# A spectral filter and two MLPs on one core: the bias written into PSUM by ScalarE, the second mixing unit in three passes, four weight conversions in the forward transform

## The chip, the core and the metric

One core of a Trainium2 chip runs the whole program in one launch. The metric is the device time of one execution in microseconds (us). The kernel before takes 1150.15 us, the median of 3 runs (1149.65 to 1151.89). TensorE (PE) multiplies, with its weight loads shown apart as PEld; VectorE (DVE), ScalarE (ACT) and GpSimd (POOL) do the elementwise work; SyncE (SP) and POOL issue DMAs.

## The reference

The input is x of shape (2, 3008, 256). Its real Fourier transform along the sequence is mixed by a complex 256x256 weight with a complex bias, soft-thresholded and transformed back; two MLPs follow (256 to 2048 to 256), one after the other.

```python
X = np.fft.rfft(x, axis=1)
Yr = Xr @ w_r - Xi @ w_i + b_r
Yi = Xr @ w_i + Xi @ w_r + b_i
Y = sign(Y) * maximum(abs(Y) - 0.01, 0)      # real and imaginary part apart
y = np.fft.irfft(Y, n=3008, axis=1)
h = x @ w_in;  x = (h * sigmoid(1.702 * h)) @ w_out       # first MLP
h = x @ w_in2; x = (h * sigmoid(h)) @ w_out2              # second MLP
```

## The kernel before

**Order.** The instructions of each engine run in the order in which the program issues them: every region opened by `region(...)` has an order written out by hand. So an instruction that waits on ACT, DVE or POOL holds back whatever stands behind it on that engine.

**Stages.** The forward transform (to some 59 us) is a product of the folded input with cosine and sine matrices, in 16 groups `(q, b, t)`: `q` is the parity of the folded rows, `b` the batch, and `t` tells even or odd frequencies (`p = t // 2`) and cosine or sine (`cs = t % 2`). The first four groups run in two pairs (`fwd_pair`), and then the loop of line 524 runs groups 4 to 15: `fwd_mm(g)` on PE, `fold(g + 3)` on DVE, the evacuation of the group before (`fwd_evac`, ACT and DVE), and, for the `g` of the list `tf`, a `tick`. `fold` and `halves` add and subtract pieces of the input; with `t == 0` both halves, sum and difference, are made (lines 323 to 337), although the difference is first read by `t == 1`. Groups 12 to 15 are evacuated through a copy `eo` on ACT (line 450) and four additions on DVE (L461, L462, L436). Every group takes two PSUM banks of a pool of four, one pool for even and one for odd groups (`bank`).

**Mixing** (59 to 131 us). Twelve units `(b, p, j)` of 128 frequencies, in `mid_mm(i)`, each with two sums of 512 columns, in the same PSUM pools. The first two units (`n32 = 2`) multiply fp32 by fp32, 16 matmul records each. The others run in three passes of fp32r with the operands split in a high and a low part: `xh` and `xl` (`xsplit`, ACT, and for `xl` a POOL DMA that adds), `wh` (L556, ACT) and `wl` (L557, DVE); 24 matmuls each. A 25th matmul, `ones` by `bias_hl` (L578), adds the bias to the first sum. `xsplit(i + 3, 1)` and `xsplit(i + 2, 0)` run two to three units ahead. `wh`, `wl` and the first splits stand after the last forward evacuation (lines 555 to 557).

**Conversion of the first MLP's weights.** They come as 64-bit numbers. One conversion is: load of 256 KB into the single buffer `raw64` (`cv_load`); absolute value on ACT (L180) into the single buffer `cv_c`; five DVE instructions (L185 to L189); a POOL DMA that adds `cv_c` to `cv_a` (L190); and, once that landed, the placing: four DVE additions (L218 to L221), four ACT instructions (L105, L107, twice) and two POOL DMAs (L106). A `tick` issues L180 of the next conversion first, then the placing of the one before, then L185 to L190, then the next load. Conversions run at `g` 6, 10 and 13 of the forward loop (`tf`), at the units of `tm` (0, 2, 4, 6, 8, 10) and at step 3 of the inverse transform (`ti`). What is converted in the later ones is kept (`hold`) and placed at the steps `pl` of the inverse.

**Inverse and MLPs.** The inverse (131 to 175 us) has 16 steps. Then 2 layers x 6 blocks of 1024 tokens x 8 weight groups run in `group`. Each group computes seven products in three passes (a Strassen-like scheme), with sums `xb[l, i, k]` of the block's quarters that are made in the last group of the block before (`xprep`). Inside `group`, `y1` is copied out of bank X by ACT (L895), and the product `prod(X, 4, 3, False)` may only be added to X once that is done; `y2` is finished by L926 and `y3` by L930. L796, `xtmp = b21 - src`, is the last step of `xprep(3)`; it reads the quarter `b11` that L895 of the next block overwrites.

Of the kernel before, what the change touches and what calls it, by code (L numbers as in the profile page):

```python
# [56 lines left out]
def spectral_mlp_kernel(ctx, tc, xin, mfwd, minv, wc, bias, w_in1, w_out1, w_in2, w_out2, outT):  # L57
# [61 lines left out]
    m_order = [("f", q, t) for q, t in ((0, 0), (0, 1), (1, 0), (1, 1), (1, 2), (1, 3), (0, 2), (0, 3))] + [("i", q, t) for q in range(2) for t in (0, 2)]  # L119
# [49 lines left out]
    def cv_bits(raw, n):  # L169
# [110 lines left out]
    raw_p = opened("raw", "left", 3)  # L280
    lv_p = opened('lv', 'left', N('lvb'))
# [20 lines left out]
    def halves(q, b, j, cs):  # L302
# [6 lines left out]
        else:  # L309
            lv = lv_p.tile([P, 2, D], F32, tag="lv", name="lv")  # L310
# [4 lines left out]
    def fold(g):  # L315
# [33 lines left out]
    def fold_pair(g):  # L349
        q, b, _ = groups[g]  # L350
        for j in range(NJ):
# [7 lines left out]
            if b == 0:  # L359
                load_raw()  # L360

    def load_wc():
        raws["wc"] = raw_p.tile([P, 4, D], F32, tag="raw", name="wc_f")
        nc.sync.dma_start(out=raws["wc"], in_=wc.rearrange("p k (h d) -> p (k h) d", h=2))
        nc.sync.dma_start(out=bias_f[0:1], in_=bias)

    def prep_wc():
# [5 lines left out]
        nc.vector.tensor_sub(bias_lo, bias_f[0:1], r32(bias_hl[0:1]))  # L373
        nc.gpsimd.dma_start(out=bias_hl[1:2], in_=bias_lo)
# [102 lines left out]
    bias_lo = wc_p.tile([1, 2 * D], F32R, name="bias_lo")  # L477
# [37 lines left out]
    load_raw(3)  # L515
# [8 lines left out]
    for g, (q, b, t) in enumerate(groups):  # L524
# [33 lines left out]

    def mid_mm(i):
# [4 lines left out]
        for grp in range(2):  # L564
            t = bank(i, "psm")
            n = 0

            for xi, off in ((0, 0), (3, D)) if grp == 0 else ((1, 0), (2, D)):
                for mm in range(2):
                    w = slice(off, off + 2 * D)  # L570
                    if hl is None:
                        nc.tensor.matmul(t, x[xi][:, mm], wc_s[:, mm, w], start=(n == 0), stop=(n == 3 and grp == 1))  # L572
                    else:
                        for k, (st, mv) in enumerate(passes(hl[xi][0][:, mm], hl[xi][1][:, mm], wh[:, mm, w], wl[:, mm, w])):
                            nc.tensor.matmul(t, st, mv, start=n == 0 and k == 0, stop=n == 3 and grp == 1 and k == 2)  # L575
                    n += 1
            if grp == 0:
# [43 lines left out]

    post = thr = None
# [27 lines left out]
    hold.insert(2, hold.pop())  # L650
# [123 lines left out]

    def xprep(l, i, k, part=3):
# [398 lines left out]
```

## Time and profile before

| | |
|---|---|
| median of 3 runs | 1150.15 us |
| the profiled execution, its own time | 1149.84 us |
| its span, first to last instruction | 1148.0 us |
| PE, PEld busy | 1138.8 us (99%), 946.3 us (82%) |
| ACT, DVE, POOL busy | 774.1, 615.5, 475.9 us (67%, 54%, 41%) |
| chain that ended last: PE | 93% |
| granted TensorE clock, mean | 1.000 |

The span is the time between the first and the last instruction, and 1.84 us of the execution lie around it. Times in the rows are microseconds from the span's start, durations of single instructions on a page are in ns. PE's ends are modelled, since matmuls overlap: the pace of matmuls is read from how far pieces of the chain lie apart and not from the length of one. A bracket after an instruction gives the idle time of its engine before it and what ended that. Short gaps on PE only show in the timeline; an engine that idles elsewhere costs nothing by itself.

### The profile page before, as it was taken

How to read it: one execution, taken by the hardware profiler on the slowest of the kernel's cores; microseconds unless marked ns; L12 is line 12 of the kernel's file. 1: busy time of each engine (PE TensorE's matmuls, PEld its weight loads, DVE VectorE, ACT ScalarE, POOL GpSimd, SP SyncE). 2: the span in 40 equal slices, each digit the busy share in tenths (PEclk: the TensorE clock that was granted, in tenths of full speed). 3: DMA queues.
4: the chain of work that ended last, by engine and by line, in shares of the span. 5: the costliest groups of instructions: out<-in, count | busy, mean ns of one | idle time of the engine just before them, and what ended most of it. 6: DMA issues, size and time to landing. Idle time of an engine off the chain costs nothing.

```text
span 1148.0 us, 14644 instructions
## 1 busy us (share of the span) xinstructions
PE 1138.8 (99%) x5094; PEld 946.3 (82%) x5094; DVE 615.5 (54%) x1015; ACT 774.1 (67%) x1445; POOL 475.9 (41%) x410
## 2 busy tenths in 40 slices
PE   8999999999999999999999999999999999999998
PEld 6768987878888888888889878888888888888897
DVE  8889997764565465564554633533523523523422
ACT  2587357877677676686677776765765866757655
POOL 0253164443444444444447646433334433344333
PEclk9999999999999999999999999999999999999999
DMA  8699494431121212112211000010000100100100
GB/s 306 176 185 238 114 161 86 105 72 37 49 62 37 74 37 59 52 38 74 52 41 37 28 28 19 1 38 1 20 18 1 37 1 1 38 1 1 37 1 33
DMA packets 39852, 68.69 MB, mean 60 GB/s; under 512 B 3681, under 2 KB 16225, under 8 KB 39778
## 3 DMA queue, kind: packets, MB, share of 16 engines
q1 hardware_dynamic: 26306, 45.51, 12.2%
q0 software_dynamic: 13472, 22.24, 11.4%
q8 instruction: 40, 0.66, 0.2%
q14 instruction: 34, 0.28, 0.1%
HBM read 35.15 MB, written 10.35 MB: 40 GB/s over the span
## 4 chain that ended last, share of the span: by engine, by line
PE 93%; DVE 2%; ACT 2%; issue 1%; DMA 1%; SPq 0%; POOL 0%; DVEq 0%; ACTq 0%; POOLq 0%
PE o L848 43%; PE x L876 37%; PE psm L575 5%; PE psi L394 4%; PE psf L394 3%; PE psm L572 1%; ACT yt L879 1%; DMA xr<-in_x 1%; ACT g L881 0%; DVE keep L313 0%; DVE tmp L796 0%; ACT yt L895 0%; ACT x L783 0%; DVE x L790 0%; SPq L485 0%
## 5 line engine op out<-in xcount | busy, mean ns | idle before, releaser
L886 POOL TENSOR_TENSOR g<-yt,g 128x512 fp32r<-128x512 f32 (+1 forms) x282 | 363.6, 1301 | 498.2 <-PE x L876 306.3
L848 PE MATMUL o<-g,wo 128*128 128x512 f32 (+1 forms) x2304 | 559.7, 385 | 0.0
L876 PE MATMUL x<-x,wi 128*128 128x512 f32 (+1 forms) x2016 | 498.9, 386 | 2.0 <-ACT yt L895 1.1
L848 PEld LDWEIGHTS o<-g,wo 128*128 128x128 f32 x2304 | 432.5, 188 | 80.6
L876 PEld LDWEIGHTS x<-x,wi 128*128 128x128 f32 x2016 | 377.5, 188 | 77.1 <-ACT yt L895 3.2
L879 ACT ACTIVATE yt<-yt 128x512 f32<-128x512 f32 (+1 forms) x288 | 179.1, 622 | 264.2 <-DVE yt L926 217.3
L881 ACT CAST g<-yt 128x512 fp32r<-128x512 f32 (+1 forms) x384 | 235.0, 612 | 12.2
L926 DVE TENSOR_TENSOR yt<-yt,x 128x512 f32<-128x512 f32 (+1 forms) x96 | 64.8, 675 | 217.7 <-PE x L876 217.3
L898 DVE TENSOR_TENSOR yt<-yt,x 128x512 f32<-128x512 f32 (+1 forms) x96 | 65.0, 677 | 175.0 <-ACT yt L895 173.1
L886 DVE TENSOR_TENSOR g<-yt,g 128x512 fp32r<-128x512 f32 (+1 forms) x102 | 70.0, 686 | 71.9 <-ACT g L881 71.9
L190 POOL DMA_DIRECT2D cv_a<-cv_c x32 | 28.1, 878 | 112.4 <-DVE cv_c L189 106.0
L930 DVE TENSOR_TENSOR yt<-yt,x 128x512 f32<-128x512 f32 (+1 forms) x96 | 64.9, 676 | 0.0
L790 DVE TENSOR_TENSOR x<-yt,x 128x512 fp32r<-128x512 f32 (+1 forms) x55 | 47.6, 866 | 31.5 <-ACT x L783 31.5
L895 ACT COPY yt<-x 128x512 f32<-128x512 f32 (+1 forms) x96 | 54.9, 572 | 1.7 <-DVE tmp L796 0.9
L879 ACT ACTIVATE yt<-x 128x512 f32<-128x512 f32 (+1 forms) x96 | 56.0, 584 | 0.0
L916 ACT COPY yt<-x 128x512 f32<-128x512 f32 (+1 forms) x96 | 55.9, 582 | 0.1
L914 ACT COPY yt<-x 128x512 f32<-128x512 f32 (+1 forms) x96 | 54.9, 572 | 1.4 <-PE x L876 1.4
L394 PE MATMUL psi<-m,f 128*128 128x188 f32 (+3 forms) x224 | 45.2, 357 | 0.0
L394 PEld LDWEIGHTS psi<-m,f 128*128 128x128 f32 x224 | 37.6, 190 | 5.5
L394 PE MATMUL psf<-m,xf 128*128 128x190 f32 (+2 forms) x176 | 36.2, 367 | 1.4 <-ACT xt L446 0.8
L394 PEld LDWEIGHTS psf<-m,xf 128*128 128x128 f32 x176 | 29.6, 190 | 8.3 <-ACT xt L446 1.3
L783 ACT CAST x<-yt 128x512 fp32r<-128x512 f32 (+1 forms) x59 | 36.4, 617 | 0.0
(120 smaller groups left out, 804.8 us busy)
## 6 DMA issues: line engine op xcount, KB each, us to landing
raw<-in_wi SPq DMA_DIRECT2D x32, 256.0 KB, 3.6
cv_a<-cv_c POOLq DMA_DIRECT2D x32, 256.0 KB, 5.0
raw<-in_wo SPq DMA_DIRECT2D x16, 512.0 KB, 3.9
xl<-xt POOLq DMA_DIRECT2D x20, 256.0 KB, 8.0
out_t<-yt SPq DMA_DIRECT2D x20, 256.0 KB, 2.0
raw<-in_x SPq DMA_DIRECT2D x9, 512.0 KB, 5.6
wi<-tmp POOLq DMA_DIRECT2D x8, 256.0 KB, 4.7
w_in<-cv_a SPq DMA_DIRECT2D x8, 256.0 KB, 2.0
```

Source lines behind the costliest of these rows:

```text
L394: nc.tensor.matmul(ps, hi[:, c : c + P], m[:, k, :w], start=i == 0, stop=i == last)
L575: nc.tensor.matmul(t, st, mv, start=n == 0 and k == 0, stop=n == 3 and grp == 1 and k == 2)
L848: nc.tensor.matmul(acc[h, mm], st, mv, start=first and k == 0, stop=last and k == 2)
L876: nc.tensor.matmul(ps, st, mv, start=first and m == 0, stop=m == 2, skip_group_check=True)
L879: nc.scalar.activation(g, g if src is None else src, func)
L881: nc.scalar.copy(gh, g)
L886: eng.tensor_sub(gl, g, r32(gh))
L895: nc.scalar.copy(y1, X)
L898: nc.vector.tensor_add(y1, y1, Y)
L916: nc.scalar.copy(y3, X)
L926: nc.vector.tensor_add(y2, y2, X)
L930: nc.vector.tensor_add(y3, y3, Z)
```

## The change

- Mixing: `n32` goes from 2 to 1, so unit 1 runs in three passes too. `xsplit(1, 1)` stands at group 10, `xsplit(2, 1)` and `xsplit(1, 0)` right behind `wl`. For units 4 to 11 ACT copies the bias from `bias_f` into the bank of the first sum one unit ahead (`put_bias`), the first matmul adds onto it (`start=False`), and the bias matmul is left out. The bias array is now 128 rows; its load of 256 KB stands at group 9, the small buffer `bias_lo` is gone.
- Forward: groups run with `t` in the order 0, 2, 1, 3; the difference half is made only when `t == 1` comes, in place in the raw tile; raw tiles 5 instead of 3, `lv` 3 instead of 6; loads are issued in another order, the last raw tile after `fold(7)`.
- Conversions: `tf` is 6, 10, 12, 14 instead of 6, 10, 13, and `ti` is empty, so four fall in the forward transform, six in the mixing, none in the inverse; `pl`, the order of `hold` and the buffers of `cv_a` follow.
- MLPs: for every block but the first L796 moves from the end of `xprep(3)` to a new `hook(7)` behind L926; `preload_act_table(AF.Silu)` stands in the first group of layer 1, behind L895.

```diff
-'tf': [6, 10, 13], 'ti': [3], 'pl': [1, 4, 8, 10, 13], 'n32': 2
+'tf': [6, 10, 12, 14], 'ti': [], 'pl': [1, 4, 8, 9, 11, 13], 'n32': 1
-    groups += [(1, b, t) for b in range(B) for t in range(4)]
+    groups += [(1, b, t) for b in range(B) for t in (0, 2, 1, 3)]
-            lv = lv_p.tile([P, 2, D], F32, tag="lv", name="lv")
+            lv = raws[q, b, j][1] if cs else lv_p.tile([P, 2, D], F32, tag="lv", name="lv")
-            if t == 0:
-                halves(q, b, j, 0)
+            if q == 1 and t < 2:
+                halves(q, b, j, t)
...
-            if t == 0:
-                halves(q, b, j, 1)
...
-    load_raw(3)
+    load_raw(6)
+    load_m()
+    load_m()
+    load_raw(2)
...
+        if g == 4:
+            load_raw()
...
+        if g == 9:
+            nc.sync.dma_start(out=bias_f, in_=bias)
         if g == 10:
-            xsplit(N('n32'), 1)
+            xsplit(1, 1)
...
     nc.vector.tensor_sub(wl, wc_s, r32(wh))
+    xsplit(2, 1)
+    xsplit(1, 0)
...
-            t = bank(i, "psm")
+            ready = i in filled and grp == 0
+            t = filled.pop(i) if ready else bank(i, "psm")
...
-            if grp == 0:
+            if grp == 0 and not ready:
                 nc.tensor.matmul(t, ones, bias_hl, start=False, stop=True)
...
+    def put_bias(i):
+        if 4 <= i < len(mids):
+            filled[i] = bank(i, "psm")
+            nc.scalar.copy(filled[i], bias_f)
...
         sd = mid_sd(*post) if post is not None else None
+        put_bias(i + 1)
...
-            if k == 3:
-                nc.vector.tensor_sub(xtmp[0], b21, src)
+            if k == 3 and not begun:
+                xfifth(l, i, src)
...
         nc.vector.tensor_add(y2, y2, X)
+        hook(7)
...
+                if h == 7:
+                    xfifth(*nxt)
...
+            if (l, i, p, h) == (1, 0, 0, 1):
+                nc.scalar.preload_act_table(AF.Silu)
```

## Rows read from the trace of the kernel before

**Rows 1.** Part 1 of the page: busy time, share of the span, instructions.
```profile
PE 1138.8 (99%) x5094; PEld 946.3 (82%) x5094; DVE 615.5 (54%) x1015; ACT 774.1 (67%) x1445; POOL 475.9 (41%) x410
```

**Rows 2.** Chain in order of time, mixing: start us, us, what.
```profile
59.59 3.43 PE psm L572 x8
...
63.25 6.87 PE psm L572 x16
...
99.51 5.45 PE psm L575 x24
...
105.19 5.45 PE psm L575 x24
...
130.63 4.39 PE psi L394 x27
```

**Rows 3.** Timeline of DVE, 18 to 25 us: start us, us, instruction, [idle before].
```profile
18.78 0.69 DVE L313 TENSOR_TENSOR lv<-raw 128x512 f32<-128x512 f32 x1
...
23.50 0.42 DVE L332 TENSOR_TENSOR xf<-lv 128x256 f32<-128x256 f32 x1
```

**Rows 4.** Timeline of PE, the same stretch.
```profile
23.98 1.24 PE L394 MATMUL psf<-m,xf 128*128 128x190 f32 x6 [0.63 <-DVE xf L332]
```

**Rows 5.** Timeline of DVE, 30 to 64 us.
```profile
44.92 0.29 DVE L218 TENSOR_TENSOR tmp<-cv_a 128x128 f32<-128x128 f32 x1 [1.65 <-DMA cv_a<-cv_c]
...
45.86 0.42 DVE L185 TENSOR_SCALAR cv_c<-cv_c 128x512 f32<-128x512 f32 x1
...
55.71 0.43 DVE L185 TENSOR_SCALAR cv_c<-cv_c 128x512 f32<-128x512 f32 x1
...
58.43 0.42 DVE L461 TENSOR_TENSOR xt<-psf,eo 128x256 f32<-128x256 f32 x1
...
61.55 1.76 DVE L557 TENSOR_TENSOR wl<-wc_s,wh 128x1536 fp32r<-128x1536 f32 x1
```

**Rows 6.** Timeline of ACT, 30 to 68 us.
```profile
55.00 0.68 ACT L180 ACTIVATE cv_c<-raw 128x512 f32<-128x512 f32 x1 [2.54 <-DMA raw<-in_wi]
...
57.44 0.83 ACT L450 COPY eo<-psf 128x376 f32<-128x376 f32 x2
...
60.04 1.48 ACT L556 CAST wh<-wc_s 128x1536 fp32r<-128x1536 f32 x1
...
62.47 1.12 ACT L507 CAST xh<-xt 128x512 fp32r<-128x512 f32 x2
64.64 0.68 ACT L180 ACTIVATE cv_c<-raw 128x512 f32<-128x512 f32 x1 [1.05 <-DMA raw<-in_wi]
```

**Rows 7.** Instructions on the tile psm: ns min/median/max, first and last start us.
```profile
L584 ACT COPY us<-psm x12: 559/568/580, 67.1 to 128.0; 128x512 f32<-128x512 f32 x12
```

**Rows 8.** Instructions of line 796, the same columns.
```profile
L796 DVE TENSOR_TENSOR tmp<-yt x11: 621/686/1786, 255.1 to 1065.9; 128x512 f32<-128x512 f32 x9, 128x448 f32<-128x448 f32 x2
```

**Rows 9.** Timeline of DVE, 247 to 272 us.
```profile
252.34 0.68 DVE L930 TENSOR_TENSOR yt<-yt,x 128x512 f32<-128x512 f32 x1
...
255.05 1.79 DVE L796 TENSOR_TENSOR tmp<-yt 128x512 f32<-128x512 f32 x1
```

**Rows 10.** Timeline of POOL, 244 to 272 us.
```profile
255.00 2.97 POOL L886 TENSOR_TENSOR g<-yt,g 128x512 fp32r<-128x512 f32 x2 [5.32 <-ACT g L881]
```

**Rows 11.** Timeline of PE, 247 to 272 us.
```profile
252.48 2.35 PE L876 MATMUL x<-x,wi 128*128 128x512 f32 x9
...
257.57 0.96 PE L876 MATMUL x<-x,wi 128*128 128x512 f32 x3 [0.69 <-ACT yt L895]
```

**Rows 12.** Timeline of PE, 636 to 674 us.
```profile
658.95 0.96 PE L876 MATMUL x<-x,wi 128*128 128x512 f32 x3 [0.26 <-ACT yt L895]
...
663.04 1.97 PE L876 MATMUL x<-x,wi 128*128 128x512 f32 x6 [0.70 <-ACT yt L916]
```

**Rows 13.** Timeline of ACT, 636 to 674 us.
```profile
658.31 0.59 ACT L895 COPY yt<-x 128x512 f32<-128x512 f32 x1 [0.88 <-DVE tmp L796]
```

**Rows 14.** A stretch of the tail: us, PE, PEld, DVE, ACT, POOL busy, PEclk, DMA share, GB/s.
```profile
1147.00:1148.00 1.00, 0.00 (x0) 0.00 (x0) 0.00 (x0) 0.00 (x0) 0.00 (x0) 0.89 0.00 0
```

More of the change, by code (lines that the diff above doesn't have):

```diff
@@ L118, in spectral_mlp_kernel @@
     m_tiles = {}
-    m_order = [("f", q, t) for q, t in ((0, 0), (0, 1), (1, 0), (1, 1), (1, 2), (1, 3), (0, 2), (0, 3))] + [("i", q, t) for q in range(2) for t in (0, 2)]
+    m_order = [("f", q, t) for q, t in ((0, 0), (0, 1), (1, 0), (1, 2), (1, 1), (1, 3), (0, 2), (0, 3))] + [("i", q, t) for q in range(2) for t in (0, 2)]
     def load_m():
@@ L172, in cv_bits @@
         c = cv_p.tile([P, 2 * CU], F32, tag="c", name="cv_c", bufs=1)
-        if n < 4:
+        if n < 3:
             a = cv_p.tile([P, 2 * CU], F32, tag="a", name="cv_a", bufs=3)
-        elif n == 4:
+        elif n == 3:
             a = cv_p.tile([P, 2 * CU], F32, tag="ld", name="cv_a", bufs=1)
@@ L279, in spectral_mlp_kernel @@
     m0_p = opened("m0", "left", 4)
-    raw_p = opened("raw", "left", 3)
-    lv_p = opened('lv', 'left', N('lvb'))
+    raw_p = opened("raw", "left", 5)
+    lv_p = opened('lv', 'left', 3)
     xs_p = opened("xs", "left", 18)
     groups = [(0, b, cs) for b in range(B) for cs in range(2)]
-    groups += [(1, b, t) for b in range(B) for t in range(4)]
+    groups += [(1, b, t) for b in range(B) for t in (0, 2, 1, 3)]
     groups += [(0, b, 2 + cs) for b in range(B) for cs in range(2)]
@@ L358, in fold_pair @@
             del raws[q, b, j]
-            if b == 0:
-                load_raw()
     def load_wc():
@@ L364, in load_wc @@
         nc.sync.dma_start(out=raws["wc"], in_=wc.rearrange("p k (h d) -> p (k h) d", h=2))
-        nc.sync.dma_start(out=bias_f[0:1], in_=bias)
+        nc.sync.dma_start(out=bias_f[0:1], in_=bias[0:1])
     def prep_wc():
@@ L372, in prep_wc @@
         nc.scalar.copy(bias_hl, bias_f)
-        nc.vector.tensor_sub(bias_lo, bias_f[0:1], r32(bias_hl[0:1]))
-        nc.gpsimd.dma_start(out=bias_hl[1:2], in_=bias_lo)
+        nc.vector.tensor_sub(bias_f[0:1].bitcast(F32R), bias_f[0:1], r32(bias_hl[0:1]))
+        nc.gpsimd.dma_start(out=bias_hl[1:2], in_=bias_f[0:1].bitcast(F32R))
     xt = {}
@@ L476, in spectral_mlp_kernel @@
     bias_hl = wc_p.tile([P, 2 * D], F32R, name="bias_hl")
-    bias_lo = wc_p.tile([1, 2 * D], F32R, name="bias_lo")
     bias_f = wc_p.tile([P, 2 * D], F32, name="bias_f")
@@ L514, in spectral_mlp_kernel @@
     fold(5)
-    load_raw(3)
     for x in prev:
@@ L571, in mid_mm @@
                     if hl is None:
-                        nc.tensor.matmul(t, x[xi][:, mm], wc_s[:, mm, w], start=(n == 0), stop=(n == 3 and grp == 1))
+                        nc.tensor.matmul(t, x[xi][:, mm], wc_s[:, mm, w], start=n == 0, stop=n == 3 and grp == 1)
                     else:
                         for k, (st, mv) in enumerate(passes(hl[xi][0][:, mm], hl[xi][1][:, mm], wh[:, mm, w], wl[:, mm, w])):
-                            nc.tensor.matmul(t, st, mv, start=n == 0 and k == 0, stop=n == 3 and grp == 1 and k == 2)
+                            nc.tensor.matmul(t, st, mv, start=n == 0 and k == 0 and not ready, stop=n == 3 and k == 2 and (ready or grp == 1), skip_group_check=ready)
                     n += 1
-            if grp == 0:
+            if grp == 0 and not ready:
                 nc.tensor.matmul(t, ones, bias_hl, start=False, stop=True)
@@ L620, in mid_fold @@
                 ft[q, b, p, -1] = ft.pop((q, b, p, 0))
+    filled = {}
+    def put_bias(i):
+        if 4 <= i < len(mids):
+            filled[i] = bank(i, "psm")
+            nc.scalar.copy(filled[i], bias_f)
     post = thr = None
@@ L649, in spectral_mlp_kernel @@
     hold.extend(settle(True))
-    hold.insert(2, hold.pop())
+    hold[2:] = hold[4:] + hold[2:4]
     cv_load(1 - len(loaded))
@@ L773, in xsums, with xfifth @@
         E('xse', 1).tensor_sub(b12, b22, b12)
+    def xfifth(l, i, src=None):
+        (b11, _), (b21, _) = xhalves(i)
+        nc.vector.tensor_sub(xtmp[0], b21, b11 if src is None else src)
     def xprep(l, i, k, part=3):
@@ L1157 @@
         "in_wc": wc,
-        "in_bias": np.concatenate([inputs["b_r"], inputs["b_i"]])[None],
+        "in_bias": np.ascontiguousarray(np.broadcast_to(np.concatenate([inputs["b_r"], inputs["b_i"]]), (P, 2 * D))),
         "in_wi1": np.ascontiguousarray(inputs["moe_w_in"]).view(np.int64),
```

7 lines of the change are left out of this document (1 added, 6 removed).

## The prediction

> **What bounds the kernel now.** I read the busy shares first, then the chain of waits in order of time, and then the timeline of each engine where the change acts. PE is busy for 1138.8 of 1148.0 us [rows 1], so an edit can only gain by taking matmuls away or by closing one of PE's few gaps, and costs whatever new gap it makes on PE. The chain through the mixing is PE alone [rows 2]: two fp32 units from 59.59, then ten units whose pieces lie 105.19 - 99.51 = 5.68 us apart, and the inverse at 130.63. A difference of 0.2% (2.3 us) is about what a measurement of this kernel can tell from no change. The sum is made against the profiled execution, 1149.84 us (span 1148.0 and 1.84 around it), which lies 0.31 below the median of the runs.
>
> **Matmuls taken away.** Of the 5.68 us of a unit the 24 matmuls take 5.45 and the bias matmul the other 0.23 [rows 2]. Eight units lose it: 8 x 0.23 = 1.84 us. Unit 1 goes from 16 fp32 records to 24 in fp32r: in the chain 16 records are 6.87 us, 24 are 5.45 [rows 2], a gain of 1.42. Together -3.26 us of PE work. The bias write costs ACT a copy of some 0.57 us [rows 7] per unit, issued right behind the copy `us` of the unit before the running one, so about a unit ahead of its reader. It writes a bank whose last reader is four units back, so it waits for nothing but ACT's own queue, and I take it at nothing. The trace has no such write into PSUM; between nothing and 8 x 0.57 = 4.6 us, were ACT late in every unit, I take nothing, as ACT has waits of its own in every unit. A gain from the write itself is excluded, since it only adds work. The larger bias load is one more DMA on SP at group 9, between loads; nobody waits for it before unit 4.
>
> **Forward transform.** At group 4 PE waits for the third folded tile, `xf` at 23.50 on DVE, and starts again at 23.98 [rows 3, 4]. Three differences of 0.69 us stand between 18.78 and that tile [rows 3]; they move to `fold(6)`. Without them its chain loses 2.0 us, of which I give 0.9 back, because the sums and their followers then depend on each other directly and can't overlap: 1.1 us earlier on PE. The last raw tile is loaded only once `fold(7)` has freed a buffer, some 5.4 us after `fold(4)` ends near 22.8 (1.0 for `fold(5)`, 4.0 for `fold(6)`, which is as long as `fold(4)` from 18.78, and 0.4), and is due four groups later on PE. I take that at nothing; if it lands late, PE loses that time ahead of unit 1, where by the next paragraph some 5 us are idle anyway. So PE would leave the forward transform at some 58.4 instead of 59.6 (unit 0 at 59.59 [rows 2]).
>
> **The fourth conversion, and what it blocks.** A tick in the loop holds ACT until the conversion before has let its buffers go. That shows at group 13: ACT stood idle for 2.54 us before L180 at 55.00, and the evacuation copies `eo` ran only after it, at 57.44 [rows 6]. The conversions come in a fixed rhythm, because each needs the landing of the DMAs of the one before: L185 stands at 45.86 and 55.71 [rows 5], and the fourth L180 at 64.64 [rows 6]. Periods are 9.85 us and, from L180 to L180, 9.64. In the kernel before this fourth one is unit 0's, behind `wh` and the first splits. In the changed one it stands at group 14, ahead of the last two evacuations, `wh`, `wl` and the splits of unit 1, and it can come hardly sooner: the first two ticks stay where they are, all of DVE's work before the second is the same, and there DVE had only 1.65 us of slack [rows 5], of which later folds and their dependences use up most. I take 0.4 us earlier, so L180 at about 64.25.
> Behind it on ACT, from the rows: L180 and the placing 2.44 (55.00 to 57.44), two `eo` 0.83, `wh` and a pair `xl` 2.43 (60.04 to 62.47), then the first `xh` 0.56 (half of 1.12) [rows 6]: 64.25 + 6.26 = 70.5. On DVE: L185 to L189 2.72 (55.71 to 58.43), from 64.97 to 67.69; two evacuations of 1.04 each (three from 58.43 to 61.55), to 69.77; `wl` 1.76, to 71.5 [rows 5]. Unit 1's first pass needs `xh` and `wh`, its second `wl`. So after one matmul it runs from 71.5, as if it had started at 71.3 without a wait.
> On PE unit 0 starts near 59.2 (its bank waits for the evacuation of group 12, behind the third conversion) and ends 7.1 us later (two halves of 3.43 and the bias 0.23), at 66.3. PE idles for some 5 us. From unit 1 on: three units of 5.68 and eight of 5.45, 60.64 us, so the inverse starts at 131.9 instead of 130.63: **+1.3 us**, where without this wait the two stages would bring 1.1 + 3.26 = 4.4. Bounds: DVE using all its 1.65 us of slack, L180 near 62.6 after somewhat quicker landings, gives -0.4; landings slower by 0.55 in each of two periods, L180 at 65.35, +2.4. I take the middle, because the DMAs are the same ones.
> Moving the later conversions and placings (none in the inverse, one placing more there) costs nothing: the inverse is PE alone in the chain, DVE loses 3.7 us of work there (44.92 to 45.86 and 55.71 to 58.43 [rows 5]), and nothing is to be gained where PE doesn't wait. At worst PE waits for the two ACT copies of the added placing, 1.2 us by a copy's 0.57 [rows 7].
>
> **Block changes of the MLPs.** L796 takes 0.69 us in most blocks but up to 1.79 [rows 8], at 255.05 [rows 9], where POOL starts two subtractions at 255.00 [rows 10]. L895 of the next block may not overwrite L796's input, so PE waits: 0.69 us at 257.57 [rows 11], and with what lies in matmul overhead 0.96 us from start to start. At the change of layers ACT idles 0.88 us for L796 [rows 13], and PE waits 0.26 and 0.70 [rows 12]. In its new place, behind L926, POOL is idle (its 5.32 us of idle time end at 255.00 [rows 10]), so L796 takes 0.69. L930, from 252.34 to 253.02 [rows 9], moves behind it, and would end near 253.65. It frees the bank of the second product of the next block, the last three of the nine matmuls from 252.48 [rows 11], due at 252.48 + 6 x 0.23 = 253.85: covered, with 0.2 us left. Without that cover each us of delay is a us of PE. Gain: 0.96 at the first, 0.88 at the change of layers (ACT's chain moves by just its idle time), together **-1.85 us**, between -1.2 and -2.3. The preload of the table takes nothing off ACT's queue, where the load stood behind L895 before too: nothing.
> The Trainium skill (SBUF — State Buffer, Who interferes with whom) says that a DVE instruction with two SBUF inputs and a GpSimd instruction that reads SBUF exclude each other for a whole instruction. The rows at 255 agree. By that rule a POOL instruction in the new place would make L796 1.79 again, L930 about 1.2 us later still, and give about 1 us of the 1.85 back; the trace has POOL idle there.
>
> **Sum.** +1.3 - 1.85 = -0.55: 1149.3 against the profile, 1149.6 against the median. Own range with the bounds above: 1147.4 to 1151.4, or 1147.7 to 1151.7 against the median.
>
> **Rivals.**
> 1. *No wait at unit 1*: the conversions come quicker, or ACT isn't held. Then 4.4 + 1.85 = 6.25 us are gained: 1143.9. For it speaks only that DVE has its folds behind it sooner; against it the L180 of rows 6, which stood 2.54 us for a landing. A partial case (L180 near 61, unit 1 some 3 us sooner than I say) gives about 1146.6.
> 2. *The clock falls in the idle piece*, and the kernel is slower. The only long idle time of PE before is the tail: no matmul runs in its last us, 1147 to 1148, and the granted clock of that us is 0.89 [rows 14], so in it TensorE went from 2.4 to 1.2 GHz. If that happens at 66 to 71 us, unit 1 starts at half pace; at the lower level each us costs 0.5 us, and for 3 us of it, which I take between nothing and the 5 us of the idle piece, as no row shows a stretch at the lower level behind one, 1.5 us are lost: 1151.1. The point from which this decides: with a fallen clock the change is slower by over 0.2% if the fourth L180 comes after 65.6, without it only after 67.1.
> The Trainium skill (TensorE: Matmul & The Clock Gate, Part 1) calls the lower level the default that activity lifts; the tail agrees, and the rule stands against every edit that opens a gap on PE.
> 3. *L796 only moves its wait*: L930 becomes late in its new order and PE waits at the second product. Then the MLP gain is under 0.9 us, 1150.6.
>
> **How the numbers follow.** Forecast with rival 3 0.40, clock fallen 0.22 (of that 0.08 over the bound), rival 1 whole 0.18, partial 0.13, something new elsewhere 0.07 (0.05 of it slower). Faster by over 0.2% (under 1147.85): 0.18 + 0.13 + 0.02 = 0.33; slower (over 1152.45): 0.08 + 0.05 = 0.13; within: 0.54. The range takes in rival 1 at its low end, for leaving both its cases out would leave 0.31: 1143.0 to 1152.5.
>
> **What the profile of the changed kernel will show.** If right: L180 near 64 us on ACT ahead of two `eo` copies and `wh`, `wl` ending near 71.5, a PE gap of 4 to 5 us around the first L575, the inverse near 131.9, no wait on L895 at the first block change, L796 at 0.69 in all blocks, and a chain whose units from 4 on are 5.45 apart. Wrong if the first L575 starts before 68, if the clock falls below 1 between 66 and 75, or if PE waits for a bias copy.

## The result and the profile after

The changed kernel takes 1158.16 us (median, 1157.05 to 1159.75), the kernel before 1150.14: a ratio of 1.007 with a 95% interval of 1.0057 to 1.0082. I had forecast 1149.6 within 1143.0 to 1152.5. It is slower, by 8.0 us. The profiled execution took 1157.05 us, with a span of 1155.3.

PE's busy time on the page answers to [rows 1]. It hardly moved, so the 7.2 us between the two profiled runs show as idle time of PE: span less busy time is 9.2 us before and 16.3 after. The line of the granted clock has one slice below 9, the third.

```profile
PE 1139.0 (99%) x5094; PEld 946.7 (82%) x5094; DVE 608.9 (53%) x1015; ACT 779.7 (67%) x1457; POOL 471.9 (41%) x412
...
PEclk9989999999999999999999999999999999999999
```

I first cut the time at three points that both traces have, the first matmul of the mixing, of the inverse and of the MLP (59.4, 130.5 and 172.4 us before; 58.5, 135.2 and 181.1 after). The forward transform ends 0.9 us sooner, the mixing takes 5.7 us more, the inverse 4.0 us more (45.9 instead of 41.9), and the MLP with all behind it, 1157.05 - 181.1 = 975.9 against 1149.84 - 172.4 = 977.4, 1.5 us less. Forward transform and MLP did what the prediction says; mixing and inverse hold the loss.

**Mixing.** The timeline of ACT, answering to [rows 6] (start us, us, instruction, [idle before]):

```profile
55.20 0.68 ACT L180 ACTIVATE cv_c<-raw 128x512 f32<-128x512 f32 x1 [6.07 <-DVE tmp L218]
...
57.63 0.83 ACT L443 COPY eo<-psf 128x376 f32<-128x376 f32 x2
65.37 0.67 ACT L180 ACTIVATE cv_c<-raw 128x512 f32<-128x512 f32 x1 [6.90 <-DMA raw<-in_wi]
...
67.80 0.82 ACT L443 COPY eo<-psf 128x376 f32<-128x376 f32 x2
68.53 1.47 ACT L552 CAST wh<-wc_s 128x1536 fp32r<-128x1536 f32 x1
69.90 1.14 ACT L496 ACTIVATE xl<-xt 128x512 fp32r<-128x512 f32 x2
70.95 1.12 ACT L500 CAST xh<-xt 128x512 fp32r<-128x512 f32 x2
...
75.01 0.69 ACT L180 ACTIVATE cv_c<-raw 128x512 f32<-128x512 f32 x1 [0.86 <-DVE tmp L218]
...
77.46 0.57 ACT L584 COPY us<-psm 128x512 f32<-128x512 f32 x1
```

The fourth conversion stands at 65.37 (forecast 64.25), and all of ACT behind it comes in the order forecast. But the last two lines are what I had not followed. The fifth conversion, started at unit 0, stands at 75.01, and only behind it comes `us`, the first copy of unit 0's result. In the kernel before that copy stood behind the fourth, and VectorE's work on units 0 and 1 followed on it. First ACT, then DVE, in the kernel before:

```profile
64.64 0.68 ACT L180 ACTIVATE cv_c<-raw 128x512 f32<-128x512 f32 x1 [1.05 <-DMA raw<-in_wi]
...
67.08 0.58 ACT L584 COPY us<-psm 128x512 f32<-128x512 f32 x1
```

```profile
68.08 0.68 DVE L586 TENSOR_TENSOR sd<-us,psm 128x512 f32<-128x512 f32 x1
...
73.89 0.69 DVE L586 TENSOR_TENSOR sd<-us,psm 128x512 f32<-128x512 f32 x1 [2.20 <-PE psm L572]
...
75.16 1.29 DVE L611 TENSOR_TENSOR f<-th 128x512 f32<-128x512 f32 x2
```

And DVE in the changed kernel:

```profile
78.45 0.68 DVE L586 TENSOR_TENSOR sd<-us,psm 128x512 f32<-128x512 f32 x1
...
83.26 1.29 DVE L611 TENSOR_TENSOR f<-th 128x512 f32<-128x512 f32 x2
```

`us` moved from 67.08 to 77.46, by 10.4 us, about one period of the conversions. Before, DVE had then to wait 2.20 us for PE's second unit; that slack is used up, and the first fold is 8.1 us late. The Trainium skill (Perfetto Trace Analysis, Tensor Engine Instruction (MATMUL, LD_WEIGHTS)) calls ACT, DVE and GpSimd strictly first in, first out; this trace agrees, for PE had finished the input of `us` by 62.4.

PE, meanwhile, waits for unit 1's operands and then runs at half pace up to 76.12; at unit 10 it waits for a bias copy:

```profile
62.18 3.60 PE L572 MATMUL psm<-wc_s,xt 128*128 128x512 f32 x8
71.60 0.79 PE L575 MATMUL psm<-wh,xh 128*128 128x512 f32 x1 [5.83 <-ACT xh L500]
72.68 0.80 PE L575 MATMUL psm<-wl,xh 128*128 128x512 f32 x1 [0.28 <-DVE wl L553]
73.27 0.63 PE L575 MATMUL psm<-wh,xl 128*128 128x512 f32 x1
73.70 0.63 PE L575 MATMUL psm<-wh,xh 128*128 128x512 f32 x1
...
76.12 0.39 PE L575 MATMUL psm<-wh,xh 128*128 128x512 f32 x1
76.34 0.39 PE L575 MATMUL psm<-wl,xh 128*128 128x512 f32 x1
...
124.22 0.50 PE L575 MATMUL psm<-wh,xh 128*128 128x512 f32 x1 [0.30 <-ACT psm L627]
```

**Inverse.** PE's timeline there, in the changed kernel; the kernel before has no such wait in this stage:

```profile
135.24 6.01 PE L387 MATMUL psi<-m,f 128*128 128x192 f32 x36
...
147.35 4.81 PE L387 MATMUL psi<-m,f 128*128 128x192 f32 x28 [0.33 <-DVE rt L429]
...
163.28 13.02 PE L387 MATMUL psi<-m,f 128*128 128x376 f32 x56 [1.53 <-issue]
176.88 4.06 PE L387 MATMUL psi<-m,f 128*128 128x376 f32 x12 [0.59 <-DVE rt L731]
181.13 0.96 PE L888 MATMUL x<-x,wi 128*128 128x512 f32 x3 [0.19 <-ACT eo L711]
```

Three of four name ScalarE or VectorE's results, and at 163.28 DVE stands behind a landing:

```profile
162.04 0.55 DVE L730 TENSOR_TENSOR ac<-rt,psi 128x377 f32<-128x377 f32 x1 [2.79 <-DMA yt<-ac]
```

The rows that tell who is late are DVE's around the mixing's last unit. Before, DVE waited for PE there, and L586 started 0.50 us after the start of PE's last matmul of the unit (130.24). After, the same L586 stands without a wait, 4.65 us after that matmul (135.01). The kernel before, then the changed one:

```profile
130.74 0.69 DVE L586 TENSOR_TENSOR sd<-us,psm 128x512 f32<-128x512 f32 x1 [0.96 <-PE psm L575]
...
135.98 1.29 DVE L611 TENSOR_TENSOR f<-th 128x512 f32<-128x512 f32 x2
```

```profile
139.66 0.68 DVE L586 TENSOR_TENSOR sd<-us,psm 128x512 f32<-128x512 f32 x1
...
144.96 1.29 DVE L611 TENSOR_TENSOR f<-th 128x512 f32<-128x512 f32 x2
146.17 0.55 DVE L719 TENSOR_TENSOR rt<-psi,eo 128x380 f32<-128x380 f32 x1
```

L719, the first sum of the inverse, stands right behind the last fold in DVE's queue, and PE needs what it frees. (An entry `x2` has two instructions; the last fold proper is the second, at 136.6 and 145.6.)

**Theory.** Two things set the end of the inverse: PE, whose work there takes 41.9 us from its first matmul, and VectorE, from whose last fold (L611) of the mixing about 35.6 us pass. These 35.6 us are not VectorE's work alone: from the fourth L722 (L730 after) of the first batch to the landing of `yt<-ac` that lets the next batch begin, 9.2 us pass before and 9.0 after, and a late fold moves that landing too. In the kernel before the two are level (130.5 + 41.9 = 172.4; 136.6 + 35.8 = 172.4). The change takes matmuls off PE, but PE starts the inverse 4.8 us late and VectorE's last fold comes 9.0 us late, because a conversion more lies ahead of the units. **Rivals**: the half clock costs the time; the moved placings make the inverse's waits; the bias copies do; the hold of unit 1's operands alone is the loss.

### The profile page after: what moved, and what is told of

It is laid out like the page before. It is cut to its first block, busy times and chain, and to the rows that moved or that the text cites. A ratio compares the mean times of both kernels' runs of the same rounds, so it can differ in the third digit from the quotient of the medians.

```text
span 1155.3 us, 14674 instructions
## 1 busy us (share of the span) xinstructions
PE 1139.0 (99%) x5094; PEld 946.7 (82%) x5094; DVE 608.9 (53%) x1015; ACT 779.7 (67%) x1457; POOL 471.9 (41%) x412
## 4 chain that ended last, share of the span: by engine, by line
PE 82%; issue 5%; ACT 2%; DVE 2%; DMA 2%; POOL 2%; POOLq 0%; DVEq 0%; ACTq 0%
PE o L860 43%; PE x L888 38%; DMA cv_a<-cv_c 1%; PE psm L575 1%; POOL xl L497 1%; ACT yt L891 1%; DMA yt<-ac 0%; DVE ac L730 0%; PE psi L387 0%; DVE x L802 0%; DVE rt L731 0%; ACT g L893 0%; ACT yt L907 0%; POOL wi L106 0%; ACT x L795 0%
## 5 line engine op out<-in xcount | busy, mean ns | idle before, releaser
L898 POOL TENSOR_TENSOR g<-yt,g 128x512 fp32r<-128x512 f32 (+1 forms) x282 | 358.2, 1281 | 502.9 <-PE x L888 313.2
L888 PE MATMUL x<-x,wi 128*128 128x512 f32 (+1 forms) x2016 | 498.5, 386 | 0.8 <-ACT yt L928 0.3
L888 PEld LDWEIGHTS x<-x,wi 128*128 128x128 f32 x2016 | 377.0, 188 | 76.4 <-ACT yt L907 2.1
L891 ACT ACTIVATE yt<-yt 128x512 f32<-128x512 f32 (+1 forms) x288 | 179.2, 622 | 264.7 <-DVE yt L938 217.7
L910 DVE TENSOR_TENSOR yt<-yt,x 128x512 f32<-128x512 f32 (+1 forms) x96 | 64.9, 676 | 181.9 <-ACT yt L907 178.5
L898 DVE TENSOR_TENSOR g<-yt,g 128x512 fp32r<-128x512 f32 (+1 forms) x102 | 70.0, 686 | 65.8 <-ACT g L893 65.8
L802 DVE TENSOR_TENSOR x<-yt,x 128x512 fp32r<-128x512 f32 (+1 forms) x55 | 43.2, 785 | 35.8 <-ACT x L795 35.8
L928 ACT COPY yt<-x 128x512 f32<-128x512 f32 (+1 forms) x96 | 55.7, 580 | 0.1
L926 ACT COPY yt<-x 128x512 f32<-128x512 f32 (+1 forms) x96 | 54.8, 571 | 1.0 <-PE x L888 1.0
L575 PE MATMUL psm<-wh,xh 128*128 128x512 f32 x88 | 35.2, 400 | 6.1 <-ACT xh L500 5.8
L180 ACT ACTIVATE cv_c<-raw 128x512 f32<-128x512 f32 x32 | 21.6, 674 | 25.1 <-DMA raw<-in_wi 10.0
```

The costliest lines, as they stand in the source:

```text
L888: nc.tensor.matmul(ps, st, mv, start=first and m == 0, stop=m == 2, skip_group_check=True)
L891: nc.scalar.activation(g, g if src is None else src, func)
L898: eng.tensor_sub(gl, g, r32(gh))
L910: nc.vector.tensor_add(y1, y1, Y)
L926: nc.scalar.copy(y2, Z)
L928: nc.scalar.copy(y3, X)
```

## The experiments

**1. Three conversions.** The changed kernel with the conversions of the kernel before.

```diff
-'tf': [6, 10, 12, 14], 'ti': [], 'pl': [1, 4, 8, 9, 11, 13]
+'tf': [6, 10, 13], 'ti': [3], 'pl': [1, 4, 8, 10, 13]
-    hold[2:] = hold[4:] + hold[2:4]
+    hold.insert(2, hold.pop())
```

> The changed kernel with the conversions of the kernel before: three in the forward transform, one in the inverse, its placings and its order of held units. All else of the change stays. Theory (the fourth conversion holds ScalarE's queue, and all that was lost follows from that): no wait ahead of unit 1 over 0.6 us, granted clock 1.0 up to the tail, inverse at 126 to 127 us in the trace, no PE wait over 0.3 us in the inverse, time 1143.9 us (1150.15 - 1.1 - 3.26 - 1.85), 1143 to 1145. Rival (the bias copies, or the new order of the folds, cost something by themselves): waits for psm near 124 us or in the forward transform stay, 1146 or more.

1150.51 us, ratio 1.0001 (0.9993 to 1.001). The wait at unit 1 is gone and the inverse starts at 127.9, 2.6 us sooner than before, yet it ends at 173.3, 0.9 later. So the fourth conversion costs 7.7 us, but taking it out doesn't bring the 6.2 forecast for the rest (1.1 + 3.26 + 1.85). PE waits 1.5 us for a bias copy at unit 4 and 2.1 us for `rt` in the inverse.

**2. Fourth conversion behind the splits.**

```diff
-'tf': [6, 10, 12, 14]
+'tf': [6, 10, 12]
...
     xsplit(2, 1)
     xsplit(1, 0)
+    tick(1)
```

> The changed kernel with the fourth conversion started behind the splits of the first units instead of at group 14; the conversions' number, the placings in the inverse and the order of the held units stay as changed. Theory (ScalarE's queue was held; the waits in the inverse are VectorE's backlog of the late mixing): both the wait of 6.4 us ahead of unit 1 and the 3.4 us of waits in the inverse go, 1143.5 to 1145.5 us. Rival (the placings at inverse steps 9 and 11 and the new order make the inverse's waits): the wait at unit 1 goes, the inverse's stay, 1147 to 1148.5 us.

1160.12 us: neither came. The wait ahead of unit 1 is gone, but a wait of 4.2 us for `xh` opens at 82.8, the last fold is at 146.9 and the inverse ends at 182.4. So a later place in ACT's queue doesn't help, as long as the fourth conversion stands ahead of the units.

**3. The idle piece filled.**

```diff
+            for _ in range(26 if (i, grp) == (0, 1) else 0):
+                nc.tensor.matmul(t, ones, bias_hl, start=True, stop=True)
```

> The changed kernel with 26 more matmuls of the bias kind (0.23 us each, 6.0 us) ahead of the second half of unit 0; their results are overwritten. PE then works through the 6 us in which it waited. Theory (the clock fell because PE stood idle): granted clock 1.0 from 5 us to the tail, unit 1 starts within 0.4 us of 71.6 as in the changed kernel, but at 0.23 us a matmul; 1.5 to 2.0 us faster than the changed kernel, 1156.4 us. Rival (the half pace of unit 1 is not due to the idle time, or the clock falls anyway): 1158.2 us.

1158.18 us, no gain, though the clock stayed up. The stretch 69 to 76 us by windows (us, PE, PEld, DVE, ACT, POOL busy, PEclk, DMA share, GB/s), in the changed kernel and with the piece filled:

```profile
69.00:76.00 7.00, 4.11 (x9) 2.94 (x10) 4.88 (x14) 6.14 (x11) 4.36 (x5) 0.51 1.07 207
```

```profile
69.00:76.00 7.00, 6.66 (x23) 4.01 (x22) 4.83 (x14) 6.09 (x12) 4.37 (x5) 1.00 1.07 209
```

So the idle time did let the clock fall, and the fall cost nothing in the end: with it cured PE waits for bias copies (2.0 us in three waits), and the last fold, 146.7, and the end of the inverse, 182.2, stay late. That rival is out.

**4. The placings moved back.**

```diff
-'pl': [1, 4, 8, 9, 11, 13]
+'pl': [1, 4, 8, 10, 13, 15]
```

> The changed kernel with the placings of the inverse at steps 1, 4, 8, 10, 13 and 15 instead of 1, 4, 8, 9, 11 and 13. Theory (the inverse's waits come from VectorE's backlog of the late mixing): waits for rt, ac and eo of 3 to 3.5 us in all stay, 1158.2 us within 0.7. Rival (the two moved placings make them): they go for the most part, 1155 to 1156 us.

1157.75 us. The placings aren't it: the inverse takes 45.3 us, against 45.9, and its waits come to 2.3 us, short of the 3 to 3.5 expected.

**5 and 6. Less work on VectorE alone**, on the version with three conversions and on the kernel before:

```diff
-        for h in range(2):
+        for h in range(2 if i < 4 else 1):
             nc.vector.scalar_tensor_tensor(out=th[:, h], ...
```

> The changed kernel with the three conversions of the kernel before, and one of the two L599 instructions (0.60 us from start to start on VectorE) left out in units 4 to 11, so that half of the threshold of these units isn't computed: 4.8 us less work on VectorE, nothing less on PE. Theory (VectorE's last fold of the mixing sets the end of the inverse): the last fold, at 137.67 us with the full work, comes 3 to 4.8 us earlier, the inverse's waits of 1.5 and 0.6 us go, and the time falls by 2.5 to 3.6 us, to 1147 to 1148. Rival (the conversions' own rhythm, landing to landing, holds the mixing): the last fold and the time stay within 1 us, 1149.5 to 1150.5.

> The kernel before with the same L599 instructions left out in units 4 to 11 (half of these units' threshold isn't computed). Theory: here PE sets the end, by some 0.2 us; VectorE's last fold comes 1 to 4 us earlier, the inverse ends at 172.2 to 172.4 as before, and the time moves by less than 0.4 us, 1149.5 to 1150.2. Rival (VectorE is the bound already before): 2 us or more are gained, 1148 or less.

1147.09 us (ratio 0.997, 0.9959 to 0.998) against 1150.51, and 1150.06 against 1150.13. The same work taken from VectorE is worth 3.4 us in one kernel and nothing in the other. Rows by line (ns min/median/max, first and last start us): L611's last start is the last fold, L888's first start (L876 in the kernel before) the end of the inverse. On three conversions, then on the kernel before:

```profile
L611 DVE TENSOR_TENSOR f<-th x22: 681/686/692, 74.4 to 134.9; 128x512 f32<-128x512 f32 x22
...
L888 PE MATMUL x<-x,wi x2016: 358/389/680, 170.6 to 1134.7; 128*128 128x512 f32 x153, 128*128 128x448 f32 x31
```

```profile
L611 DVE TENSOR_TENSOR f<-th x22: 682/686/692, 75.5 to 136.4; 128x512 f32<-128x512 f32 x22
...
L876 PE MATMUL x<-x,wi x2016: 358/389/678, 172.7 to 1138.9; 128*128 128x512 f32 x153, 128*128 128x448 f32 x31
```

On three conversions fold and end came 2.8 and 2.7 us sooner (than 137.7 and 173.3), the fold just short of the 3 us expected. On the kernel before, the fold was hardly earlier, against my 1 to 4 us: VectorE still waits there for PE's last unit.

**7. The same on the changed kernel.**

> The changed kernel with one of the two L599 instructions left out in units 4 to 11 (half of these units' threshold isn't computed): 4.8 us less on VectorE, PE's work and the held ScalarE queue ahead of unit 1 as they are. Theory (the inverse's 4 us of waits are VectorE's lateness; the rest of the loss is the held queue): the wait of 6 us at unit 1 and the inverse's start near 135.2 stay, the inverse takes 41.9 us as before instead of 45.9, time 1154.0 to 1155.0 us. Rival (the inverse's waits come from elsewhere): 1158 us.

1154.69 us. Last fold 143.6, end 179.1; the inverse takes 43.5 us, not quite the 41.9 of PE alone. So at least 3.5 of the 8 us are VectorE's lateness beyond PE's; 1.6 us beyond PE's 41.9 are left even here. The rest is PE's late start of the inverse (4.8 us), less what the MLP gains.

**8. One conversion less in the mixing**, with four ahead of it.

```diff
-'tm': [0, 2, 4, 6, 8, 10], 'ti': []
+'tm': [2, 4, 6, 8, 10], 'ti': [3]
```

> The changed kernel with the conversion at unit 0 of the mixing taken out and one at step 3 of the inverse put back, with the placings and the order of the kernel before: four conversions ahead of the mixing, five in it, one in the inverse. Theory (each conversion started ahead of the units holds them for a period): the wait of 6 us at unit 1 stays, but VectorE's folds come 4 to 8 us sooner than in the changed kernel, the last by 141, so PE sets the inverse's end (start near 135, 41.9 us of work): 1153.5 to 1155 us. Rival (the waits of the inverse have nothing to do with how many conversions lie ahead of it): 1158 us.

1154.39 us (ratio 1.0026, 1.0014 to 1.0038), as expected, but not by the way expected: the first fold stayed at 83.2, and the last came at 144.0, only 1.6 us sooner. The traced executions differ by 1.9 us, the medians by 3.8, so the traces account for half of that gain. `us` of unit 0, no longer behind a conversion, was at 74.8 instead of 77.5. But VectorE's queue then stood for unit 1, which PE had started late:

```profile
81.97 0.69 DVE L586 TENSOR_TENSOR sd<-us,psm 128x512 f32<-128x512 f32 x1 [2.55 <-PE psm L575]
...
83.23 1.28 DVE L611 TENSOR_TENSOR f<-th 128x512 f32<-128x512 f32 x2
```

So there are two holds side by side, and unit 1's operands by themselves put the first fold at 83.2.

**9. The four conversions alone**, on the kernel before (the edit of 1, the other way round).

> The kernel before with the four conversions in the forward transform alone, with the placings and the order that go with them; units 0 and 1 stay fp32 and need neither wh nor the splits. Theory (the conversions run in a fixed rhythm, and one more of them ahead of the units puts VectorE's whole mixing back by most of a period): first fold of unit 0 at 82 to 84 us instead of 75.2, last fold 7 to 9 us late, 1156 to 1159 us. Rival (only the hold of unit 1's operands costs, and PE has unit 1's 6.9 us of fp32 to cover it): at most 2 us slower, 1150 to 1152 us.

1157.50 us, ratio 1.0064 (1.0049 to 1.0079): as much slower as the whole change. Unit 1 is fp32 here and PE doesn't wait for it at 66 to 72 us; still the first fold is at 84.8 and the last at 147.2, later than expected. ACT twice, then DVE:

```profile
76.60 0.67 ACT L180 ACTIVATE cv_c<-raw 128x512 f32<-128x512 f32 x1 [2.94 <-DVE tmp L218]
...
79.04 0.57 ACT L584 COPY us<-psm 128x512 f32<-128x512 f32 x1
84.84 1.28 DVE L611 TENSOR_TENSOR f<-th 128x512 f32<-128x512 f32 x2
```

So the other hold, unit 0's `us` behind the fifth conversion, is by itself enough as well, and the loss comes without a bias copy and without unit 1's operands: those two rivals are out as its only cause. Either hold puts the first fold 8 to 10 us back, and the changed kernel has both; the prediction saw the first alone.

**10. The bias write alone**, on the kernel before.

```diff
+            filled[i] = bank(i, "psm")
+            nc.scalar.copy(filled[i], bias_f)
```

> The kernel before with the bias write alone (ScalarE writes the bias of units 4 to 11, the larger bias load). Theory (PE and VectorE are level in the mixing): the eight bias matmuls' 1.84 us come back as waits of PE for VectorE or for the bias copy; inverse starts up to 1.8 us earlier, ends within 0.4 us of 172.4, 1149.5 to 1150.5 us. Rival (the prediction's: PE alone is the path): 1148.0 to 1148.4 us.

1150.32 us, ratio 1.0 (0.9989 to 1.0012). Of the 1.84 us nothing shows in the median. Its trace by itself proves little, since in that execution the forward transform ended 1.6 us late (61.1), which takes up the gain on PE; experiments 13 and 14 show it cleaner.

**11. L796 moved, alone**, on the kernel before.

```diff
         nc.vector.tensor_add(y2, y2, X)
+        hook(7)
...
+                if h == 7:
+                    xfifth(*nxt)
```

> The kernel before with L796 alone moved into its new place behind the second product's sum (units, conversions, table load as before). The prediction's step: PE waits of 0.96 us at the first block change and 0.88 at the change of layers go, 1148.3 us, 1147.9 to 1149. Rival (L930, now behind it, is late for the second product): within 0.9 us of the kernel before.

1148.28 us, ratio 0.998 (0.9971 to 0.999), as the prediction has it; the rival falls.

**12. Two conversions in the inverse, five in the mixing.**

```diff
-'tm': [0, 2, 4, 6, 8, 10], 'ti': [3]
+'tm': [0, 2, 4, 6, 8], 'ti': [1, 5]
```

> The changed kernel with three conversions in the forward transform, five in the mixing (units 0, 2, 4, 6, 8) and two in the inverse (steps 1 and 5), the first placings in order. Looked for: a faster one. Theory: VectorE's last fold comes some 3 us sooner than the 137.67 of the version with three, six and one; what is gained is up to 3.6 us less VectorE's 3.6 us for the second conversion in the inverse, where 2.5 us of its time were idle: 1147.5 to 1149.5 us. Rival (the conversions in the inverse hold its sums as much as in the mixing): 1150.5 us or more.

1156.08 us, a miss. PE waits 2.9 us for a bias copy, and in the inverse 5.1 us for `eo`, which stands behind an L180 held until 158.4: the same hold in a new place.

**13 and 14. What keeps three conversions from gaining.** Unit 1 back in fp32; then, with the second edit, the bias matmuls back as well.

```diff
-'n32': 1
+'n32': 2
...
-        if 4 <= i < len(mids):
+        if False:
```

> The version with three conversions in the forward transform, and besides unit 1 back in fp32 (its splits with it); the new forward transform, the bias write and the moved L796 stay. Theory A (the splits of unit 1, ahead of the unit loop on ScalarE, put the mixing's conversions back by the 2.9 us that showed with three passes): L180 of unit 0 near 64.5 us instead of 67.5, last fold at 135 to 136.5, end of the inverse 35.6 later, 1146.5 to 1148 us. Rival B (the new forward transform itself makes the third conversion late, 56.6 instead of 55.0 us, and the mixing follows): L180 near 67, last fold near 137.7, 1150 to 1150.8 us.

> As the version with unit 1 in fp32, and the bias added by matmuls in every unit again: of the change the new forward transform and the moved L796 are left (with the table load and the larger bias load). Looked for: a version faster than both kernels, and the forward transform's own worth. If VectorE's folds come earlier with the forward transform (theory A): inverse starts 1.0 us earlier than in the kernel before, 1146.9 to 1147.6 us. If the third conversion is late because of it (rival B): no gain beside L796's, 1148 to 1149 or, with the last fold at 137.7, 1150.

1147.67 us (ratio 0.9972, 0.9962 to 0.9982) and 1147.91 (0.9981, 0.9972 to 0.999). Both beat both kernels. L180 of unit 0 came at 65.35 instead of 67.5, so theory A holds for 2.2 of its 2.9 us: the splits of the three-pass unit put the conversions back. The last fold, 136.7, is just behind the 136.5 expected at most, and 1147.91 just above the 1146.9 to 1147.6 expected of the second. The rows by line of the first, then of the second (L611 is L608 here, L888 is L885):

```profile
L608 DVE TENSOR_TENSOR f<-th x22: 681/686/694, 74.2 to 136.7; 128x512 f32<-128x512 f32 x22
...
L885 PE MATMUL x<-x,wi x2016: 358/389/680, 172.3 to 1136.3; 128*128 128x512 f32 x153, 128*128 128x448 f32 x31
...
L387 PE MATMUL psi<-m,f x224: 320/325/583, 127.6 to 180.3; 128*128 128x188 f32 x44, 128*128 128x192 f32 x32, 128*128 128x376 f32 x24, 128*128 128x190 f32 x12
```

```profile
L608 DVE TENSOR_TENSOR f<-th x22: 682/687/693, 74.2 to 135.6; 128x512 f32<-128x512 f32 x22
...
L885 PE MATMUL x<-x,wi x2016: 362/389/678, 171.4 to 1135.7; 128*128 128x512 f32 x153, 128*128 128x448 f32 x31
...
L387 PE MATMUL psi<-m,f x224: 320/325/479, 129.5 to 179.6; 128*128 128x188 f32 x44, 128*128 128x192 f32 x32, 128*128 128x376 f32 x24, 128*128 128x190 f32 x12
```

With the bias write PE starts the inverse 1.9 us sooner, the eight bias matmuls to within a tenth, and ends it 0.9 later: most of it is given back as waits for `rt` (0.8 and 0.6 us), and the last fold is 1.1 us later.

**All runs under the two rules.** Columns: first matmul of the inverse, last fold, first product of the MLP (the end), each read from rows like those above; then what PE's rule (start + 41.9) and the fold's (last fold + 35.6) make of the end; the median. The two constants were read from these same traces. The first three columns are of one traced execution each, which lies up to 2.6 us from the median of all runs (1160.06 us for the four conversions alone, 1148.84 for 1).

| kernel | inverse | fold | end | by PE | by fold | median us |
|---|---|---|---|---|---|---|
| before | 130.5 | 136.6 | 172.4 | 172.4 | 172.2 | 1150.1 |
| before, less on DVE | 130.8 | 136.4 | 172.7 | 172.7 | 172.0 | 1150.1 |
| bias write alone | 130.2 | 136.5 | 172.2 | 172.1 | 172.1 | 1150.3 |
| L796 alone | 130.9 | 137.0 | 172.8 | 172.8 | 172.6 | 1148.3 |
| forward, L796 (14) | 129.5 | 135.6 | 171.4 | 171.4 | 171.2 | 1147.9 |
| 14 and bias write (13) | 127.6 | 136.7 | 172.3 | 169.5 | 172.3 | 1147.7 |
| 13 and unit 1 in three passes (1) | 127.9 | 137.7 | 173.3 | 169.8 | 173.3 | 1150.5 |
| 1, less on DVE | 127.5 | 134.9 | 170.6 | 169.4 | 170.5 | 1147.1 |
| after | 135.2 | 145.6 | 181.1 | 177.1 | 181.2 | 1158.2 |
| after, less on DVE | 135.6 | 143.6 | 179.1 | 177.5 | 179.2 | 1154.7 |
| one less in mixing | 136.6 | 144.0 | 179.6 | 178.5 | 179.6 | 1154.4 |
| placings back | 135.1 | 144.9 | 180.3 | 177.0 | 180.5 | 1157.8 |
| idle piece filled | 136.3 | 146.7 | 182.2 | 178.2 | 182.3 | 1158.2 |
| fourth later | 137.4 | 146.9 | 182.4 | 179.3 | 182.5 | 1160.1 |
| four conversions alone | 136.4 | 147.2 | 182.8 | 178.3 | 182.8 | 1157.5 |
| two in inverse | 131.0 | 138.1 | 182.1 | 172.9 | 173.7 | 1156.1 |

In fifteen of sixteen the later of the two rules gives the end within 0.3 us; the sixteenth has its own wait, named in 12. The runs with less work on VectorE make the fold's rule more than a coincidence of two things that move together: there PE's work is untouched.

The last fold follows the start of the mixing's conversions. In the fourteen kernels with six of them in the mixing, 68.7 to 72.0 us pass from L180 of unit 0 to the last fold, whether three or four conversions stand ahead, with the bias matmuls or without. A late start is not made up. Nor is it VectorE's amount of work that paces the mixing, for of the 4.8 us taken from it only 2.8 and 2.0 us show at the last fold (5 and 7). Whether the conversions' landings or PE's own pace do, these runs leave open: ten units of PE take 54.5 us without the bias matmul and 56.8 with it, and the six conversions, from the first L180 to the last, 53.8 to 56.9.

## Why the prediction was wrong, point by point

- **What bounds the kernel.** "An edit can only gain by taking matmuls away or by closing one of PE's few gaps" left out the second bound. The chain [rows 2] is PE alone, but by little: at the last unit VectorE waited for PE for only 0.96 us. That row of the kernel before was there to be read; by it, an estimate, 4.4 us less on PE could bring no more than about 1 us there, unless VectorE came sooner too.
- **Matmuls taken away, -3.26.** The 1.84 of the bias came on PE to within a tenth (127.6 against 129.5), and in the time nothing of it shows (13 against 14, with intervals that overlap). The three passes of unit 1, -1.42, cost in place of gaining: 1150.51 against 1147.67 in the medians, 1.2 us between the traced executions. The bias copy taken "at nothing" was waited for: PE idled 0.3 us for it in the changed kernel, 1.5 in experiment 1.
- **Forward transform, -1.1.** Right on PE: unit 0 starts 0.9 us sooner; in the trace of experiment 14 inverse and end come 1.0 sooner than before. In the time it isn't shown: the ratio is 0.998 with L796 alone (11) and 0.9981 with both (14).
- **The fourth conversion, +1.3.** The step that failed, in two ways. Its mechanism at unit 1 was right, but its terms came out larger: the second matmul at 72.68 instead of 71.5 (L180 1.1 us later than forecast, at the end of the bounds given), 1.6 us for the lower clock, as the eight steps from the start at 72.68 to that at 76.12 take 3.44 us instead of 1.82 (rival 2, its size about as forecast), and 0.6 us, with the slower starts around it, at the bias copy of unit 10. That makes the inverse's start 135.2 instead of 131.9. And the step stopped at PE. It didn't ask what VectorE does once unit 1 is late, and it left out the tick at unit 0, which now starts the fifth conversion with `us` of unit 0 behind it, though the last of [rows 6] is that very tick with the fourth. Experiment 8 isolates the first, experiment 9 the second, at 7.4 us.
- **"Moving the later conversions and placings (none in the inverse, one placing more there) costs nothing: the inverse is PE alone in the chain".** The inverse became 4.0 us longer. DVE does lose the fourth conversion's work there, as the step says, but its queue reaches the inverse 9 us late.
- **MLP blocks, -1.85.** Right. 1157.05 - 181.1 against 1149.84 - 172.4 is 1.5 us less, experiment 11 gives 1.9 in its trace (1148.29 - 172.8 = 975.5) and 1.6 in the median. PE's waits behind 185 us, 1.8 us before (for L895 and L916), are 0.3 after, at 670.15 for L928; experiment 11, without the moved table load, has none, so the preload taken at "nothing" may cost these 0.3 us. L796, now L785, takes at most 0.69 us:

```profile
L785 DVE TENSOR_TENSOR tmp<-yt x11: 619/685/689, 261.3 to 1070.3; 128x512 f32<-128x512 f32 x9, 128x448 f32<-128x448 f32 x2
```

That answers to [rows 8], and rival 3 fell. The rule of the Trainium skill on VectorE and GpSimd (SBUF — State Buffer, Who interferes with whom) is in agreement: at the first block change POOL idles for 5.53 us up to 263.94, and L785 at 261.26 takes 0.68.
- **Rivals and range.** Rival 2 came, but as a part: experiment 3 takes the fallen clock away and the time stays. The true cause, VectorE's late last fold as the bound, was no rival at all; DVE stood in the text only as something that gets less to do. The point from which a slowdown starts, the fourth L180 after 65.6, was nearly reached (65.37), and would alone have given some 1152. Two of its signs of being wrong came, the fallen clock and the wait for a bias copy. Its own range isn't the sum of its bounds: -0.4 to +2.4 and -2.3 to -1.2 give 1147.1 to 1151.0 against the profile, not 1147.4 to 1151.4; the measured time lies far outside either.

## What to carry to other kernels

When one engine is busy 99% of the time, look for the place where another engine last waited for it, and how long: 0.96 us of DVE at the mixing's last unit was about all that PE's savings could buy. When a step is moved ahead in a queue that works in order, follow not only what it pushes back but every later step that is started at a fixed place: here each of them met one conversion more. And an engine that is ahead gives no sign on its own: half the clock at the start of unit 1 cost 1.6 us on PE and nothing in the time, since VectorE's last fold was later still.

## What the runs showed of the hardware

- PE idled from 65.8 to 71.6 us. TensorE's granted clock was 1.00 up to 69 us, 0.50 from 70 to 75 (1.2 of 2.4 GHz), 0.51 over 69 to 76 in the mean, and 1.00 again from 76; matmuls started 0.43 us apart up to 75.83 and 0.23 apart from 76.12. With the idle piece filled it was 1.00 throughout. The Trainium skill (TensorE: Matmul & The Clock Gate, Part 1) calls the lower level the default; the trace agrees.
- Experiment 10's profiled execution had the lower level behind shorter waits: PE waited 1.1 and 0.6 us between 21 and 24 us, and the mean granted clock of the next 4 us was 0.57, while in the kernel before, with waits of 0.8 and 0.6 us at that place, it was 1.00. What made the difference isn't shown. By windows, experiment 10 and the kernel before:

```profile
24.00:28.00 4.00, 4.00 (x15) 4.00 (x16) 3.97 (x12) 0.60 (x3) 0.00 (x0) 0.57 0.95 324
```

```profile
24.00:28.00 4.00, 4.00 (x25) 4.00 (x26) 3.97 (x12) 1.37 (x8) 0.00 (x0) 1.00 0.98 293
```

- The accumulating DMA of 256 KB that ends a conversion took 3.3 to 8.5 us from issue to landing in the changed kernel (median 5.2), and it can be the larger part of a conversion's period in the mixing. L180 stood at 109.55 and 121.32, and the landing between them is in the chain of waits:

```profile
113.51 7.79 DMA cv_a<-cv_c
```
